# Two linear-attention layers with ReGLU MLPs on one core: another plan of the same work, token tiles of adjacent rows, stores on two queues, a padded weight

## The chip, the cores and the metric

The kernel runs on one core of a Trainium2 chip. The metric is the device time of one execution in microseconds (us); lower is better. The engines are named as in the profile: PE (TensorE's matmuls; PEld is its weight loads), DVE (VectorE), ACT (ScalarE), POOL (GpSimd) and SP (SyncE, which here only issues transfers).

## The reference

The input is a sequence of 2048 tokens of 512 values in bfloat16. Two rounds with the same weights are computed, each an attention block A and an MLP block B with residual additions:

```python
def A(x):                                   # linear attention, H = 32 heads of Dh = 16
    q, k, v = split(x @ wqkv)
    phi = lambda u: concat([softmax(u @ w_phi), softmax(-(u @ w_phi))])   # per head
    kv, z = sum_s phi(k)^T v, sum_s phi(k)
    return (phi(q) @ kv / (phi(q) @ z + 1e-6)) @ wo
def B(x):                                   # MLP, F = 1376
    gate, up = x @ W_gate, x @ W_up
    return (relu(gate) * up) @ W_down
for _ in range(2):
    x = x + A(layernorm(x)); x = x + B(layernorm(x))
```

The sum over all tokens in A means that no query of a round can be finished before all keys of that round are done. Everything else goes token by token.

## The kernel before, in words

**Tiles.** The tokens are cut into 16 tiles of 128 rows (`T`, `P`), which stay in SBUF as X for the whole run. Before the change, four tiles make a group `c`, and partition `p` of the group holds four neighbouring tokens, one in each tile (`xv`, `ov`, lines 285 and 286). A pair of tiles is loaded with one transfer.

**Operations.** Nothing is ordered by loops. The function builds a list of 1855 operations (`op`), numbered by when they are created, each with an engine, what it depends on, and the buffers that it takes and uses. Four tables written out above it hold a plan that was made beforehand: `ORDER` (line 185) is the order in which all of them are emitted, and with it the order in each engine's own queue; `SLOTS` (161) says which buffer of a pool each operation takes; `PLACE` (155) says, for each operation that two engines could do (`alt`), which one does it; `IDLE` (173) puts dummy matmuls ahead of PE operations (the fifth PE operation gets one). `arrange` (76) only replays the plan. An engine works through its queue in order, so an operation that waits holds back all behind it on that engine.

**Stages.** For each tile: load, layer norm statistics (line 500), scaling (522 on POOL, 524 on DVE), transposition (485 by a transfer for a pair of tiles, 490 on PE for a single tile), keys K (581), values V (586), exponentials on ACT (564), their sums on DVE (591), scaling on POOL or DVE (551), and the accumulation over all tokens `kvz` (614). Queries Q (641) go the same way and are transposed by a transfer (666). When all tiles' keys are summed, the state R is built on DVE (626, 631) and the attention of each tile runs: `erq` (677), division (684 to 691), transposition `oT`, output product (700), residual (704). The MLP runs in blocks of 1, 1, 2, 4, 4 and 4 tiles: centring (720), transposition, gate and up products (777; the last 96 of the 1376 columns apart, 753), relu on ACT (781), the product of the two on DVE, either straight from PSUM (794) or after a copy on ACT (796, 785), then the down product (817) and the residual (824). The weights wk and wq are folded with `w_phi` at the start (463, 471).

**The down product.** W_down has 1376 = 10 x 128 + 96 rows, so its 11th slice has 96 rows in `wd`, and the 11th matmul of each tile contracts over 96 partitions (`m`, line 816). The 11th slice of the other operand comes out of a transposition of `hr`, whose last 32 columns are set to zero at the start (`hr0`, line 403).

**Transfers.** All loads, stores and transpositions are issued by SP, but for the load of the first x tile and of w_phi, which ACT issues. They take eight semaphores, the counters, in turn: a transfer can be issued when the one eight places earlier in the list has landed. The first transfers of SP's queue before are: x2, wk (first half), x1, x4-5, wk (second half), x3, wv, wv, x6-7, x8-9, x12-13, wq, wq, then the transposition of tiles 4 and 5, Wq's two, the transposition of tiles 12 and 13, x10-11, x14-15 (xN is the load of tile N). The other weights follow between transpositions. At the end, each tile is stored when its residual is done (890); the last tile in two parts of 384 and 128 columns. The queue of SP ends with a transposition for the last MLP block and then 13 stores.

Of the kernel before, what the change touches and what calls it, by code (L numbers as in the profile page):

```python
# [8 lines left out]
P = 128  # L9
D = 512  # L10
# [135 lines left out]
class K:  # L146
# [9 lines left out]
    "1001001010001001101010000101111000001001111100100001101100111011000011000000100000101111011100010100"  # L156
    "1001101111010010110000010110000011011001111010011101100111110011110011001111111010011101111101011001"
    "1100011011011000110101111111111101111110010101011000010100100001101000100101111100010011011001010100"
    "1010110010011111000100110101101001100101100011101100100"
)  # L160
SLOTS = (
    "0001450332111040002521331020252213134130241204554001324122142118332305232454002133223601357001146113"
    "37331110214c1029215b124e344a030f050d1609305j031g253c321b012i144h204k360a1200050401151502000212011020"
    "2400001150000020350210121400102105010002500401004005212214201851002313115213501425303231310500410142"
    "1024202011521574410443221121100401010352431312302242101240511013402460230322025003051301002510502000"
    "1042222135013132244254224011350135402481030275405k21311041150211321401210232450232222330131532542063"
    "2110112025213310385404e052f313d2459131i320j201b062b154f210c145a3509160h004d212e331g12011301020313001"
    "0124302000035011021540000124501002145001012230210000111041011030210121231001501441322200001041042225"
    "0420351321112001514214224324413412402523105223205102100110050000220551450552131532232412541321040123"
    "1130421000550542551212451342421030015034"  # L170
# [3 lines left out]
    0, 0, 0, 0, 1,  # L174
# [100 lines left out]
)  # L275


@with_exitstack
def kernel(
# [22 lines left out]
    def x_of(t):  # L302
        return X[t // C][:, t % C, :]
# [632 lines left out]
```

## Time and profile before

| what | value |
|---|---|
| time, median of 3 runs | 369.18 us (368.44 to 369.18) |
| profiled execution's own time | 368.89 us |
| its span, first to last instruction | 367.1 us |
| PE busy, matmuls | 360.5 us (98%), 2589 |
| DVE, ACT, POOL busy | 267.8, 188.2, 71.4 us |
| bytes moved by DMA | 31.70 MB |
| granted TensorE clock | 0.999 |

The span is what the trace covers; the time of an execution is a little longer. Busy time is the time in which an engine works on an instruction; waits, and the issuing of transfers, are not in it. A row of a timeline gives the start, the length, the engine with the line, the operation, what it writes and reads, and in brackets the engine's idle time ahead of it with what ended it. A row of groups gives the count, the busy time, the mean of one in ns, and the idle time ahead with what ended it.

### The profile page before, as it was taken

What the parts mean: (1) busy time and instruction counts of PE and PEld (TensorE: products, weight loads), DVE (VectorE), ACT (ScalarE), POOL (GpSimd) and SP (SyncE); (2) the same over time, 40 slices, a digit from 0 to 9 for tenths busy, and PEclk for the clock granted to TensorE, in tenths of its full rate; (3) what the DMA queues carried; (4) which work ended last, traced back from release to release, by engine and by line L of the source; (5) the groups of instructions that cost most, each with busy time, mean ns of one, the idle gap of its engine ahead of it and who ended that gap; (6) DMA issues with size and microseconds to landing.
All of it is one profiled execution on the core that took longest, in us unless ns stands there. A gap on an engine that the chain in (4) does not pass through costs nothing.

```text
span 367.1 us, 6928 instructions
## 1 busy us (share of the span) xinstructions
PE 360.5 (98%) x2589; PEld 199.2 (54%) x2589; DVE 267.8 (73%) x607; ACT 188.2 (51%) x530; POOL 71.4 (19%) x101
## 2 busy tenths in 40 slices
PE   8999999999999999999999999999999999999994
PEld 4445568786545444444544556776755444454442
DVE  6999999998887247958789898899756745251342
ACT  6899998361434633414883375863423441434220
POOL 6579831210010001000208363010300000000000
PEclk9999999999999999999999999999999999999999
DMA  7987776466730600041110206346652210200025
GB/s 246 214 208 203 192 163 130 90 127 134 116 71 18 131 10 3 1 100 30 29 42 3 57 4 145 45 77 147 145 119 57 63 30 0 57 2 14 0 59 173
DMA packets 92994, 31.70 MB, mean 86 GB/s; under 512 B 85184, under 2 KB 91168, under 8 KB 92960
## 3 DMA queue, kind: packets, MB, share of 16 engines
q1 hardware_dynamic: 92288, 31.11, 38.1%
q8 instruction: 20, 0.33, 0.4%
q10 hardware_dynamic: 672, 0.15, 0.2%
q14 instruction: 14, 0.11, 0.1%
HBM read 8.44 MB, written 2.10 MB: 29 GB/s over the span
## 4 chain that ended last, share of the span: by engine, by line
PE 93%; DMA 3%; DVE 2%; issue 0%; ACTq 0%; SPq 0%; ACT 0%
PE b L777 38%; PE b L817 21%; PE b L700 8%; PE b L641 7%; PE b L586 6%; PE b L581 6%; PE b L753 3%; PE q L614 2%; PE q L677 2%; DMA X<-in_A_x_dram 2%; DMA wf<-in_A_w_phi_dram 1%; DVE bstA L500 1%; PE b L490 1%; DVE sk L591 1%; DVE X L824 0%
## 5 line engine op out<-in xcount | busy, mean ns | idle before, releaser
L777 PE MATMUL b<-xnTB,wgu 128*128 128x512 bf16 (+2 forms) x960 | 150.7, 308 | 0.0
L777 PEld LDWEIGHTS <-wgu 128*128 128x128 bf16 x960 | 80.3, 98 | 57.4 <-issue 0.2
L781 ACT ACTIVATE gu<-b 128x512 bf16<-128x512 f32 (+1 forms) x82 | 47.9, 589 | 100.0 <-PE b L777 93.6
L817 PE MATMUL b<-wd,hT 128*128 128x512 bf16 (+3 forms) x363 | 84.1, 372 | 0.0
L564 ACT ACTIVATE ek<-b 128x480 bf16<-128x480 f32 x128 | 68.2, 585 | 11.4 <-PE b L641 7.0
L794 DVE TENSOR_TENSOR hT<-gu,b 128x512 bf16<-128x512 bf16 (+1 forms) x53 | 35.1, 663 | 36.3 <-PE b L777 19.8
L551 POOL TENSOR_TENSOR ek<-ek 128x480 bf16<-128x480 bf16 x40 | 39.2, 1008 | 94.2 <-ACT ek L603 93.9
L817 PEld LDWEIGHTS <-hT 128*128 128x128 bf16 (+1 forms) x363 | 34.5, 98 | 37.4
L591 DVE TENSOR_REDUCE sk<-ek 128x64 f32<-128x960 bf16 x32 | 36.1, 1143 | 1.8 <-ACT ek L564 0.9
L646 DVE TENSOR_REDUCE sq<-ek 128x64 f32<-128x960 bf16 x32 | 36.4, 1144 | 0.0
L662 POOL TENSOR_TENSOR ek<-ek 128x480 bf16<-128x480 bf16 x18 | 18.3, 1020 | 87.2 <-DVE ek L657 56.6
L700 PE MATMUL b<-wo,oT 128*128 128x512 bf16 x128 | 31.4, 379 | 0.0
L586 PE MATMUL b<-wv,xnTA 128*128 128x512 bf16 x128 | 31.4, 379 | 0.0
L824 DVE SCALAR_TENSOR_TENSOR X<-b,rsB,X 128x512 bf16<-128x512 f32 (+2 forms) x33 | 23.8, 727 | 9.0 <-PE b L817 8.6
L581 PE MATMUL b<-Wk,xnTA 128*128 128x480 bf16 x128 | 30.2, 366 | 0.0
L641 PE MATMUL b<-Wq,xnTA 128*128 128x480 bf16 x128 | 30.1, 365 | 0.0
L691 DVE TENSOR_TENSOR o<-q,rd 128x512 bf16<-128x512 f32 x32 | 22.0, 689 | 10.0 <-ACT rd L688 9.7
L785 DVE TENSOR_TENSOR hT<-gu 128x512 bf16<-128x512 bf16 x29 | 12.1, 421 | 21.0 <-ACT gu L796 21.0
L796 ACT CAST gu<-b 128x512 bf16<-128x512 f32 x29 | 17.0, 586 | 16.2 <-PE b L777 15.4
L704 DVE SCALAR_TENSOR_TENSOR X<-b,X 128x512 bf16<-128x512 f32 x32 | 22.0, 686 | 3.5 <-PE b L700 3.3
L500 DVE BATCH_NORM_STATS2 bstA<-X 128x6 f32<-128x512 bf16 x32 | 21.3, 682 | 2.1 <-DMA X<-in_A_x_dram 2.0
L700 PEld LDWEIGHTS <-oT 128*128 128x128 bf16 x128 | 12.2, 98 | 13.2
(77 smaller groups left out, 328.8 us busy)
## 6 DMA issues: line engine op xcount, KB each, us to landing
out_dram<-X SPq DMA_DIRECT2D x15, 128.0 KB, 2.2
X<-in_A_x_dram SPq DMA_DIRECT2D x6, 256.0 KB, 4.7
wgu<-in_B_W_gate_dram SPq DMA_DIRECT2D x4, 344.0 KB, 3.4
wgu<-in_B_W_up_dram SPq DMA_DIRECT2D x4, 344.0 KB, 4.0
wd<-in_B_W_down_dram SPq DMA_DIRECT2D x5, 256.0 KB, 3.9
hT<-in_A_wqkv_dram SPq DMA_DIRECT2D x4, 256.0 KB, 5.3
wv<-in_A_wqkv_dram SPq DMA_DIRECT2D x2, 256.0 KB, 4.5
wo<-in_A_wo_dram SPq DMA_DIRECT2D x4, 128.0 KB, 4.0
```

The source lines that it names most:

```text
L551: e.tensor_tensor(out=v[:, :, 0:DF, :], in0=v[:, :, 0:DF, :], in1=spread(ek, v, n), op=Alu.mult)
L564: nc.scalar.activation(out=pairs(ek, s)[:, :, 0:DF, :], in_=ps.t[:, 0:FW].rearrange("p (b f h) -> p b f h", h=2, f=DF), func=AF.Exp, scale ...
L581: k = op("PE", mm(4, FW), due, lambda: [nc.tensor.matmul(kp.t[:, 0:FW], lhsT=xnTA[c][:, i, b, :], rhs=Wk2[:, b, :], start=(b == 0), stop=( ...
L586: v = op("PE", mm(4, 512), due_v, lambda: [nc.tensor.matmul(vp.t[:], lhsT=xnTA[c][:, i, b, :], rhs=wv[:, b, :], start=(b == 0), stop=(b == ...
L591: a = op("DVE", SUM16, due, lambda: nc.vector.tensor_reduce(out=sk.t[:, row, :].rearrange("p (b h) -> p b h", h=2), in_=summed(pairs(ek)), ...
L641: q = op("PE", mm(4, FW), due, lambda: [nc.tensor.matmul(qp.t[:, 0:FW], lhsT=xnTA[c][:, i, b, :], rhs=Wq2[:, b, :], start=(b == 0), stop=( ...
L646: a = op("DVE", SUM16, due, lambda: nc.vector.tensor_reduce(out=sq.t[:].rearrange("p (b h) -> p b h", h=2), in_=summed(pairs(ek)), axis=AX ...
L700: a = op("PE", mm(4, 512), due + 3, lambda j=j, yp=yp: [nc.tensor.matmul(yp.t[:], lhsT=oT.t[:, j, b, :], rhs=wo[:, b, :], start=(b == 0), ...
L777: nc.tensor.matmul(ps.t[:, q * W:(q + 1) * W].rearrange("p (i t) -> p i t", t=P), lhsT=wgu[:, s, b, g * P:(g + 1) * P], rhs=xT.t[:, 0:n, b ...
L781: nc.scalar.activation(out=gu.t[:, 0, 0:cols], in_=gp.t[:, 0:cols], func=AF.Relu)
L794: nc.vector.tensor_tensor(out=h.t[:, f0 * W:f0 * W + cols], in0=gu.t[:, 0, 0:cols], in1=up.t[:, 0:cols], op=Alu.mult)
L817: nc.tensor.matmul(yp.t[:, 0:c1 - c0], lhsT=h.t[:m, f * W + i * P:f * W + (i + 1) * P], rhs=wd[:m, f, c0:c1], start=(f == 0), stop=(f == N ...
```

## The change

It has four parts.

1. Tile `t` holds the tokens 128 t to 128 t + 127, partition `p` one of them. A pair of tiles is still loaded with one transfer, now of two runs of 1 KB a partition in place of one of 2 KB.
2. The last 32 rows of the 11th slice of `wd` are set to zero by a DVE memset at the start, a new operation (number 25; those behind it move up by one), and all down products contract over 128 partitions and wait for the memset.
3. A store may be issued by ACT or by SP; the choice is in `PLACE`. In the new plan ten of the 17 stores are on ACT and seven on SP. The last eight in emission order are, SP: tile 12, tile 8, tile 14, the last 128 columns of tile 15; ACT: tile 9, tile 13, tile 10, the first 384 columns of tile 15.
4. `ORDER`, `SLOTS`, `PLACE` and `IDLE` are those of another plan, in whose making the eight counters of the transfers were taken into account. The number of matmuls, the dummies among them, is the same.

Read out of the new lists: SP's queue begins x2, x1, wk (first half), x4-5, wk (second half), wv, wv, x3, x12-13, x6-7, x8-9, wq, x10-11, wq, wo (last block), then the transposition of tiles 4 and 5, Wq's first, x14-15, Wq's second. The block weights (`Wblk`, line 419) are built on DVE, not on POOL. The dummy matmul stands ahead of the second PE operation. Behind the folding of wk, PE's first products are V, K of tiles 2, 0 and 1 mixed with V of tile 1, tile 3's turn, V of tile 0, K and V of tile 3, then K of tile 5; before, K of tile 4 came at this place after the same nine products. The first `kvz` stands behind the keys of tiles 12 and 13. In round 2, two query products stand between the last `kvz` and the first `erq` (before: one); in round 1, two query products, a turn and an `erq` stand between the first output product and the first turned MLP tile (before: one query product, a turn and an `erq`).

```diff
-    xv = xf.rearrange("(c p i) d -> c p i d", c=C, i=C)
-    ov = of.rearrange("(c p i) d -> c p i d", c=C, i=C)
+    xv = xf.rearrange("(t p) d -> p t d", p=P)
+    ov = of.rearrange("(t p) d -> p t d", p=P)
...
-        o = load(due, X[t // C][:, t % C:t % C + n, :], xv[t // C][:, t % C:t % C + n, :], n * 131072, eng, follow, t < 1)
+        o = load(due, X[t // C][:, t % C:t % C + n, :], xv[:, t:t + n, :], n * 131072, eng, follow, t < 1)
...
+    wd_zero = op("DVE", dve(D, 4), 9500, lambda: nc.vector.memset(wd[FR:P, NF - 1, :], 0.0), name="wd0", port=True)
...
-                            m = min(P, F - f * P)
-                            nc.tensor.matmul(yp.t[:, 0:c1 - c0], lhsT=h.t[:m, f * W + i * P:f * W + (i + 1) * P],
-                                             rhs=wd[:m, f, c0:c1], start=(f == 0), stop=(f == NF - 1))
+                            nc.tensor.matmul(yp.t[:, 0:c1 - c0], lhsT=h.t[:, f * W + i * P:f * W + (i + 1) * P],
+                                             rhs=wd[:, f, c0:c1], start=(f == 0), stop=(f == NF - 1))
...
-                              [made[f] for f in range(lo, hi)] + l_wd + ([last] if lo else []),
+                              [made[f] for f in range(lo, hi)] + l_wd + [wd_zero] + ([last] if lo else []),
...
-                    op("SP", (460, 1700), e0, lambda t=t, c0=c0, c1=c1: nc.sync.dma_start(
-                        out=ov[t // C][:, t % C, c0:c1], in_=x_of(t)[:, c0:c1]), [a], name="store",
-                       move=256 * (c1 - c0) / RATE)
+                    ways = [(e, (460, 1700), lambda q=q, t=t, c0=c0, c1=c1: q.dma_start(
+                        out=ov[:, t, c0:c1], in_=x_of(t)[:, c0:c1]), False)
+                            for e, q in (("SP", nc.sync), ("ACT", nc.scalar))]
+                    op(*ways[0][:2], e0, ways[0][2], [a], name="store", move=256 * (c1 - c0) / RATE, alt=ways[1])
...
 ORDER = (
-    1, 16, 5, 29, 7, 8, 25, 0, 4, 20, 19, 28, 10, 9, 6, 82, 3, 83, 46, 2, 21, 11, 18, 30, 26, 22, 47, 32, 12, 17, 84,
...
+    1, 16, 5, 30, 7, 4, 20, 22, 25, 18, 21, 19, 0, 26, 8, 10, 9, 3, 83, 2, 47, 6, 84, 65, 48, 31, 27, 14, 66, 28, 33,
...
 IDLE = (
-    0, 0, 0, 0, 1,
+    0, 1,
```

More of the change, by code (lines that the diff above doesn't have):

```diff
@@ L155 @@
 PLACE = (
[L156 to L159, printed above, removed]
+    "1001000111111011000010000100111100001000011010000011101110101011000110000001000000101101011000001100"
@@ L160 @@
+    "0110001001010011111100101011000000111001001000001101100111100001101010011000101100001100000111000001"
+    "1011010110100110100001111011011000111010010010010101010001001100011111110111100000001001111101110110"
+    "001001111010011001101001110101111111111001101010101111010111000011101010"
 )
 SLOTS = (
-    "0001450332111040002521331020252213134130241204554001324122142118332305232454002133223601357001146113"
-    "37331110214c1029215b124e344a030f050d1609305j031g253c321b012i144h204k360a1200050401151502000212011020"
@@ L164 @@
[L164 to L168, printed above, removed]
@@ L169 @@
-    "0420351321112001514214224324413412402523105223205102100110050000220551450552131532232412541321040123"
-    "1130421000550542551212451342421030015034"
+    "0001543042112102002542113023000115435300453012414205023302011148532213102333434443220614217523155121"
+    "08000150024a001c3109124d032b244h052g161k205d020i365a310c235f152e343j10290100020401111302000234011020"
+    "2300001123000020030210120400102131010002200403001004421210201011302514111013311025401624210500320011"
+    "2110325301052112003722221100131221542240331050312501451230550152540280400241122412323032001100114202"
@@ L171 @@
+    "52400250422501351301031110502140205225544012k5334j01121150111321430422342332200212440410251551302045"
+    "0023302141224104580332b320k060h234g104a253c045d115g064b134e323c040h361f212a3339151i00011501020411001"
+    "0120202000001011021040000125301002131001012530210005020000042013150023041111421340201521000142052015"
+    "2520151454210510114112302222413522311200103200421032410210131120411230512210501530250502311235110112"
+    "0031101050542121030250012251221421014230"
 )
```

176 rows, old and new, of the table ORDER are left out of this document.

## The prediction

> **What bounds the kernel now.** I read the page's totals and its 40 slices first, then the chain that ended last, then PE's waits, then the first 20 us and the last 10 us row by row.
>
> ```profile
> span 367.1 us, 6928 instructions
> PE 360.5 (98%) x2589; PEld 199.2 (54%) x2589; DVE 267.8 (73%) x607; ACT 188.2 (51%) x530; POOL 71.4 (19%) x101
> PE   8999999999999999999999999999999999999994
> PE 93%; DMA 3%; DVE 2%; issue 0%; ACTq 0%; SPq 0%; ACT 0%
> ```
>
> TensorE is busy for 360.5 of 367.1 us and makes up 93% of the chain. Only the first and the last slice are not full. The table by stretches says the same more sharply (columns: length, busy PE, PEld, DVE, ACT, POOL, clock, DMA share, GB/s):
>
> ```profile
> 20.00:58.00 38.00, 38.00 (x324) 20.74 (x322) 36.56 (x64) 37.05 (x113) 25.55 (x30) 1.00 0.79 193
> 58.00:220.00 162.00, 162.00 (x1101) 88.74 (x1098) 129.81 (x288) 79.00 (x233) 25.85 (x27) 1.00 0.28 58
> 220.00:234.00 14.00, 13.93 (x161) 8.43 (x159) 11.42 (x25) 9.27 (x25) 3.89 (x4) 1.00 0.52 114
> 234.00:352.00 118.00, 118.00 (x838) 66.97 (x836) 68.40 (x180) 46.55 (x117) 4.36 (x4) 1.00 0.29 60
> ```
>
> From 20 to 352 us PE is idle for 0.07 us by this view, at the granted clock of 1.00 (the ends of matmuls are modelled, so shorter waits show only in the starts, as in part 4). In 20 to 58 us ACT (37.05 of 38.00) and DVE (36.56) are nearly full too, so a late operand there has no spare engine to catch up on. All PE waits that the view of waits lists:
>
> ```profile
> PE q L437 <- PEq L920: 0.8, 1, 0.8
> PE b L490 <- POOL xn L522: 0.5, 1, 0.5
> PE b L471 <- ACT rsA L510: 0.4, 1, 0.4
> PE q L614 <- DVE ek L551: 0.3, 1, 0.3
> ```
>
> So a new order can win only in three places: the start, a few small waits, and the tail after the last matmul. It can lose anywhere. The profiled execution took 368.89 us, 1.79 us more than its span; the three runs have 369.18, 369.18 and 368.44. I sum against 368.89 and carry the 1.79 over; the median is 0.29 us (0.08%) above it.
>
> **Part 1: W_down padded to 128 rows.** These two groups are the last slice of the down products (96 rows) and the others:
>
> ```profile
> L817 PE MATMUL b<-wd,hT 128*128 128x512 bf16 x310 | 77.2, 379 | 0.0
> L817 PE MATMUL b<-wd,hT 96*128 96x512 bf16 x31 | 11.8, 381 | 0.0
> L403 DVE MEMSET hr<- 128x64 uint32 x2 | 0.2, 112 | 0.0
> 354.27 7.65 PE b L817 x38
> ```
>
> Both take the same (379 and 381 ns), and in the chain's last run, 38 down products of which every eleventh has 96 rows take 7.65 us without a break. The columns don't change, so PE gains 0. The added memset writes 512 elements in 32 partitions; by L403's 112 ns for 64 words (256 words here) it is 0.1 to 0.45 us of DVE, before 2 us, where DVE has no tile to work on. The new dependence of every down product on it was met 60 us earlier. Cost 0; without that cover it is the memset's own time.
>
> **Part 2: work moved between engines.** Decoded from the two lists, the copies of V that ACT makes go from 20 to 27 of 32, the copies of Up from 29 to 35 of 82, the query scalings on POOL from 18 to 13.
>
> ```profile
> L443 ACT CAST vext<-b 128x512 bf16<-128x512 f32 x20 | 11.6, 599 | 2.0 <-PE b L586 2.0
> L796 ACT CAST gu<-b 128x512 bf16<-128x512 f32 x29 | 17.0, 586 | 16.2 <-PE b L777 15.4 <-ACT gu L796 0.6
> L662 POOL TENSOR_TENSOR ek<-ek 128x480 bf16<-128x480 bf16 x18 | 18.3, 1020 | 87.2 <-DVE ek L657 56.6 <-issue 25.8 <-ACT gr L758 4.8
> ```
>
> ACT gains about 7 x 0.60 + 6 x 0.59 = 7.7 us and ten stores; POOL loses 5.1. Summing the same way over the first layer's keys and queries alone, ACT, DVE and POOL each change by 1 us or less, so the full stretch (20 to 58 us) is not loaded more. The rest lies where ACT is busy for 79 of 162 us. Cost 0, hidden by that idle ACT; if some of it lay ahead of a product that PE needs next, each copy costs up to 0.6.
>
> **Part 3: the start.** PE's first useful work and the first product that needs a transposed tile from the DMA queue:
>
> ```profile
> 4.64 0.62 PE L463 MATMUL b<-ident,hT 128*128 128x128 bf16 x8
> 9.06 1.03 PE L586 MATMUL b<-wv,xnTA 128*128 128x512 bf16 x4
> 10.02 1.34 SPq L485 DMA_TRANSPOSE xnTA<-xn  x1
> 15.91 0.57 PEld L581 LDWEIGHTS <-xnTA 128*128 128x128 bf16 x4 [0.27 <-DMA xnTA<-xn]
> 15.97 0.97 PE L581 MATMUL b<-Wk,xnTA 128*128 128x480 bf16 x4
> DMA to landing us min/median/max: 2.3/2.7/5.8
> ```
>
> The last row is from the view of the tile xnTA. The first transposition (tiles 4 and 5) is issued at 10.02 and is the one with the longest landing, 5.8 us, so about 15.85; the load of its weights (15.91) names it as the releaser. It lands late because it stands behind loads in SP's queue. In the new list two more loads stand ahead of it: x tiles 10 and 11 (256 KB) and the last block of wo (128 KB). What 384 KB cost is in these stretches:
>
> ```profile
> 6.20:8.70 2.50, 2.13 (x29) 1.63 (x28) 2.50 (x7) 2.49 (x10) 2.30 (x5) 1.00 1.01 338
> 8.70:11.80 3.10, 3.10 (x24) 1.67 (x22) 2.61 (x6) 2.88 (x8) 1.96 (x5) 1.00 1.17 348
> ```
>
> 393 KB at 348 bytes per ns is 1.13 us. The x pairs, 2 KB runs before and 1 KB runs after, add little: the first stretch lands 1 KB runs at 338, the second mostly 2 KB runs at 348, 3% of 0.75 us for each of five pairs, 0.1 us. The transposition then lands near 17.1.
>
> When does PE need it? Both lists have the same nine K and V products and one turned tile between the first V product (9.06) and this point (15.97). Ahead of that, wk's first half is issued one place later and x1 one earlier, DVE builds the block weights instead of POOL, and POOL is freed for the tiles: followed row by row, the first V product comes at 8.9 to 9.0, within -0.2 to +0.5 of before. So PE arrives near 16.0 and **waits 1.1 us**. What goes is the wait of the first kvz, which now stands behind five more products:
>
> ```profile
> 19.45 0.43 PE L614 MATMUL q<-vext,ek 128*128 128x65 bf16 x8 [0.30 <-DVE ek L551]
> ```
>
> The one spare dummy matmul moves from the fifth to the second PE operation, where PE waits for wk in both: 0. The start's net is +1.1 - 0.3 - 0.1 = **+0.7 us**. Bounds: -0.6 (the transposition isn't held up, and the fold is earlier) and +2.6 (it and the next ones each come later, see the rivals). I take the value by the DMA row, since PE runs in order and nothing that it could do meanwhile stands ahead of the waiting product.
>
> **Part 4: two small waits.** Layer 2's first attention product follows the state R, one query product after the last kvz; layer 1's first turned MLP tile follows its centring:
>
> ```profile
> 225.62 0.97 PE L641 MATMUL b<-Wq,xnTA 128*128 128x480 bf16 x4
> 226.67 0.41 PE L677 MATMUL q<-R,fq 128*128 128x68 bf16 x8
> 55.78 0.97 PE L641 MATMUL b<-Wq,xnTA 128*128 128x480 bf16 x4
> 56.72 0.40 PE L490 MATMUL b<-ident,xn 128*128 128x128 bf16 x4
> ```
>
> Four query matmuls occupy 4 x 0.2025 = 0.81 us (480 columns at 2.4 per ns plus 2.5 ns), so PE was late by 226.67 - 226.43 = 0.24 and 56.72 - 56.59 = 0.13. In the new list one more query product stands in the first gap, and one more query in the second. **-0.35 us.** Counting, for each PE operation, the PE work since its last PE ancestor less the durations on the way, the old list has two places with 0.03 us to spare behind the start, the new one has none under 0.3. That speaks against new waits in the middle, but leaves out queueing on ACT and DVE: I hold 0 to +1.5 us for it, and take 0.
>
> **Part 5: the tail.** The last two additions on DVE, and the stores on SP (the second row from the view of line 890, the last one a stretch):
>
> ```profile
> 361.94 0.97 DVE L824 SCALAR_TENSOR_TENSOR X<-b,rsB,X 128x384 bf16<-128x384 f32 x2 [0.39 <-PE b L817]
> L890 SPq DMA_DIRECT2D out_dram<-X x13: 333/420/512, 357.7 to 363.8; - x13
> 357.69 6.47 SPq L890 DMA_DIRECT2D out_dram<-X  x13
> 357.00:366.00 9.00, 5.52 (x36) 2.87 (x34) 3.13 (x5) 0.00 (x0) 0.00 (x0) 1.00 0.54 177
> ```
>
> The last addition ends at 362.91, but the last store is issued at 363.8 (363.75): SP works through 13 stores at 6.47 / 13 = 0.50 us each. After, the last eight stores are split, four on SP and four on ACT. Between the tiles of the last two on SP lie 7 matmuls of 384 and 11 of 128 columns, 1.7 us, so SP is free when the last addition ends and issues within 0.04 us instead of 0.84: **-0.8 us**, bounds -0.5 and -1.1. ACT's four stand behind its last MLP work, with nothing behind them. Its six earlier ones each hold it for about as long as an issue on SP (420 ns); by the list the additions that they wait for come well before, and the transfer eight places earlier, whose counter each of them shares, has landed. ACT is idle enough there (46.55 busy of 118 us).
>
> The Trainium skill speaks against spreading stores: "DMA: Bandwidth & Descriptors", section "Issuing engines are not separate DMA queues", says that issuing from several engines only saves the sequencer's issue time, since all share the same DMA engines. Here the DMA engines are busy for 0.54 of 357 to 366 us, so the trace agrees that the issue is the limit, and by the rule the sum stays at -0.8. If movement were the limit the tail would give 0.
>
> **Sum.** 368.89 + 0.7 - 0.35 - 0.8 = 368.4 us (span 366.65).
>
> **Rivals.**
> - *The transposition is not late* (chance 0.20). The queue's extra loads overlap its wait for its own tile, or land faster. For it: 5.8 us is far over the 2.7 median, so part may be its own. Then the start gives -0.4: 368.89 - 0.4 - 0.35 - 0.8 = 367.3.
> - *The crowded queue costs more than one wait* (0.28), the other side. Behind the first transposition stand Wq's two, with x tiles 14 and 15 (256 KB, 0.75 us) now between them; if the first lands at 19.0 (+3.0) the fold of Wq and the next keys wait too. Start +2.6: 368.89 + 2.6 - 0.35 - 0.8 = 370.3. It decides from a landing of 17.6 on (start +1.15), where the gains are used up. For it: PE has no slack here. Against: 1.13 us by the bandwidth row.
> - *The tail doesn't shorten* (0.12): the stores' movement, not their issue, ends the run. 368.89 + 0.7 - 0.35 = 369.2. Against: 0.54 above.
>
> **How the numbers follow.** Forecast 0.40, rivals 0.20, 0.28, 0.12. About 0.2% (0.74 us) is what a measurement of this kernel tells from no change, so faster means under about 368.4 and slower over 369.9. The forecast lies on that line: half of it counts as faster, half as the same. Faster: 0.20 + 0.20 = 0.40. Same: 0.20 + most of the tail's case, 0.10, less than 0.02 of it slower: 0.29. Slower: 0.28 and the rest, 0.31. Range: the first rival's 367.3 less 0.3 for the tail's bound gives 367.0; the second's 370.3 with a little of the middle's bound gives 370.6. Forecast's own range 367.9 to 369.1.
>
> **What would show it.** The first key product on tiles 4 and 5 waits about 1 us near 16 to 17 for a DMA; the kvz wait is gone; no wait ahead of L677 near 226; the last store is issued within 0.1 us of the last addition and the span ends about 3.4 us after it (now 367.1 - 362.91 = 4.2); PE's busy time stays at 360.5. A PE wait of over 0.3 us anywhere between 20 and 352, or a start over 1.2 us later, proves me wrong.

## The result, and the profile after

The changed kernel takes 367.36 us (median of 13 runs, 366.64 to 368.52), the kernel before 368.83 us beside it (13 runs, 368.28 to 369.18). The ratio is 0.9963, 95% interval 0.9952 to 0.9974: faster by 1.47 us. The profiled execution took 366.92 us. Lines of the changed kernel are one higher than before from L407 to L813.

The totals, PE's slices and the chain of the changed kernel's page:

```profile
span 365.1 us, 6937 instructions
PE 360.0 (99%) x2589; PEld 199.4 (55%) x2589; DVE 266.8 (73%) x613; ACT 190.7 (52%) x540; POOL 62.1 (17%) x93
PE   8999999999999999999999999999999999999996
PE 93%; ACT 2%; DMA 2%; DVE 2%; issue 0%; POOL 0%; POOLq 0%
```

PE still bounds the kernel and its busy time is the same to 0.5 us; the span is 2.0 us shorter. The last slice is fuller (6, was 4). The waits of PE in the changed kernel:

```profile
PE b L582 <- DMA xnTA<-xn: 0.8, 1, 0.8
PE q L438 <- PEq L921: 0.8, 1, 0.8
PE b L464 <- DMA hT<-in_A_wqkv_dram: 0.3, 1, 0.3
PE b L472 <- DVE hT L445: 0.2, 1, 0.2
```

The wait of the first kvz is gone. New are one for a transposed tile and one for W_k's load (hT is the buffer that W_k is loaded into). Where they lie, in PE's rows of the changed kernel:

```profile
5.55 0.62 PE L464 MATMUL b<-ident,hT 128*128 128x128 bf16 x8 [0.35 <-DMA hT<-in_A_wqkv_dram]
8.80 1.03 PE L587 MATMUL b<-wv,xnTA 128*128 128x512 bf16 x4
15.72 0.97 PE L582 MATMUL b<-Wk,xnTA 128*128 128x480 bf16 x4
20.64 1.19 PE L582 MATMUL b<-Wk,xnTA 128*128 128x480 bf16 x5 [0.78 <-DMA xnTA<-xn]
224.73 1.78 PE L642 MATMUL b<-Wq,xnTA 128*128 128x480 bf16 x8
226.35 0.42 PE L678 MATMUL q<-R,fq 128*128 128x68 bf16 x8
```

The key product on tiles 4 and 5 (15.72) does not wait; the one on tiles 12 and 13 (20.64) does. The transposition of tiles 4 and 5 was issued at 10.70 and landed at 14.67. Its view, and that of the load of W_k's first half (issued at 1.66, landed at 5.50):

```profile
L486 SPq DMA_TRANSPOSE xnTA<-xn x1: 1338/1338/1338, 10.7 to 10.7; - x1
DMA to landing us min/median/max: 4.0/4.0/4.0
```

```profile
L351 SPq DMA_DIRECT2D hT<-in_A_wqkv_dram x1: 427/427/427, 1.7 to 1.7; - x1
DMA to landing us min/median/max: 3.8/3.8/3.8
```

Eight query matmuls take 8 x 0.2025 = 1.62 us, so the attention product at 226.35 is on time: the wait of 0.24 is gone. The stretches that answer to those of before:

```profile
20.00:58.00 38.00, 37.36 (x327) 20.75 (x328) 35.99 (x60) 36.53 (x110) 23.90 (x28) 1.00 0.70 177
58.00:220.00 162.00, 162.00 (x1107) 88.87 (x1104) 125.71 (x288) 84.86 (x248) 21.30 (x22) 1.00 0.33 67
220.00:234.00 14.00, 14.00 (x162) 8.59 (x160) 12.65 (x24) 9.92 (x25) 1.93 (x2) 1.00 0.00 1
234.00:352.00 118.00, 118.00 (x832) 66.92 (x830) 70.24 (x189) 42.89 (x113) 1.98 (x2) 1.00 0.35 69
357.00:366.00 9.00, 5.11 (x34) 2.71 (x32) 3.78 (x6) 0.00 (x0) 0.00 (x0) 1.00 0.31 102
```

PE is full from 58 to 352 us, the 0.07 us near 226 included; the DMA's share in the last stretch fell from 0.54 to 0.31, since stores that stood there now go earlier.

The tail of the changed kernel (last additions, the last stores on SP, the last one on ACT; then the view of the very last store):

```profile
361.53 0.96 DVE L824 SCALAR_TENSOR_TENSOR X<-b,rsB,X 128x384 bf16<-128x384 f32 x2 [0.39 <-PE b L817]
358.15 4.71 SPq L890 DMA_DIRECT2D out_dram<-X  x4
362.18 0.34 ACTq L890 DMA_DIRECT2D out_dram<-X  x1
```

```profile
L890 SPq DMA_DIRECT2D out_dram<-X x1: 333/333/333, 362.5 to 362.5; - x1
DMA to landing us min/median/max: 1.5/1.5/1.5
```

The same view of the last store of the kernel before:

```profile
L890 SPq DMA_DIRECT2D out_dram<-X x1: 405/405/405, 363.8 to 363.8; - x1
DMA to landing us min/median/max: 2.3/2.3/2.3
```

The last addition ends at 362.49, the last store is issued at 362.53 and landed at 364.01. Before: 362.91, 363.75, 366.01. From addition to issue 0.84 became 0.04, and from issue to landing 2.26 became 1.48.

**The books of one execution.** PE's lost time is, for each matmul, the distance to the next start less its columns at 2.4 per ns. I sum it over the matmuls that start in the first 40 us ("start") and later ("middle"); "tail" is from the last matmul's start to the end of the span. Before: start 5.09, middle 7.22, tail 4.80. After: 5.21, 6.68, 3.21. So +0.1 - 0.5 - 1.6 = -2.0 us, the difference of the spans. This pair differs by 0.5 us more than the medians (-1.47); why comes out below.

### The profile page after: what moved, and what is told of

Same layout as the page of the kernel before. It is cut to its first block, busy times and chain, and to the rows that moved or that the text cites. A ratio compares the mean times of both kernels' runs of the same rounds, so it can differ in the third digit from the quotient of the medians.

```text
span 365.1 us, 6937 instructions
## 1 busy us (share of the span) xinstructions
PE 360.0 (99%) x2589; PEld 199.4 (55%) x2589; DVE 266.8 (73%) x613; ACT 190.7 (52%) x540; POOL 62.1 (17%) x93
## 4 chain that ended last, share of the span: by engine, by line
PE 93%; ACT 2%; DMA 2%; DVE 2%; issue 0%; POOL 0%; POOLq 0%
PE b L778 38%; PE b L817 21%; PE b L701 8%; PE b L642 7%; PE b L587 6%; PE b L582 6%; PE b L754 3%; PE q L678 2%; PE q L615 2%; DMA xnTA<-xn 1%; DVE bstA L501 1%; DMA X<-in_A_x_dram 1%; ACT ek L565 1%; PE b L491 1%; ACT Wk L444 0%
## 5 line engine op out<-in xcount | busy, mean ns | idle before, releaser
L782 ACT ACTIVATE gu<-b 128x512 bf16<-128x512 f32 x82 | 47.4, 586 | 95.2 <-PE b L778 94.1
L817 PE MATMUL b<-wd,hT 128*128 128x512 bf16 (+2 forms) x363 | 84.1, 372 | 0.0
L552 POOL TENSOR_TENSOR ek<-ek 128x480 bf16<-128x480 bf16 x38 | 36.6, 989 | 129.9 <-DVE ek L552 99.9
L817 PEld LDWEIGHTS <-hT 128*128 128x128 bf16 x363 | 34.4, 98 | 36.7
L795 DVE TENSOR_TENSOR hT<-gu,b 128x512 bf16<-128x512 bf16 (+1 forms) x47 | 31.2, 671 | 31.2 <-PE b L778 22.1
L797 ACT CAST gu<-b 128x512 bf16<-128x512 f32 (+1 forms) x35 | 19.7, 574 | 9.0 <-PE b L778 8.9
L786 DVE TENSOR_TENSOR hT<-gu 128x512 bf16<-128x512 bf16 (+1 forms) x35 | 14.2, 408 | 13.4 <-ACT gu L797 13.4
L663 POOL TENSOR_TENSOR ek<-ek 128x480 bf16<-128x480 bf16 x13 | 12.8, 987 | 40.8 <-DVE ek L658 20.3
```

The costliest lines, as they stand in the source:

```text
L552: e.tensor_tensor(out=v[:, :, 0:DF, :], in0=v[:, :, 0:DF, :], in1=spread(ek, v, n), op=Alu.mult)
L782: nc.scalar.activation(out=gu.t[:, 0, 0:cols], in_=gp.t[:, 0:cols], func=AF.Relu)
L795: nc.vector.tensor_tensor(out=h.t[:, f0 * W:f0 * W + cols], in0=gu.t[:, 0, 0:cols], in1=up.t[:, 0:cols], op=Alu.mult)
L817: nc.tensor.matmul(yp.t[:, 0:c1 - c0], lhsT=h.t[:, f * W + i * P:f * W + (i + 1) * P], rhs=wd[:, f, c0:c1], start=(f == 0), stop=(f == NF ...
```

## The experiments

My first theory: the layout made the landings shorter, so that the first transposition wasn't late (L). Rivals: the second issuing queue shortened the tail's landing too (Q), or the new order did it all (O). Each run's ratio is to the kernel before beside it; an interval behind a ratio is at 95%.

**1. All stores back on SP.**

```diff
-                            for e, q in (("SP", nc.sync), ("ACT", nc.scalar))]
+                            for e, q in (("SP", nc.sync), ("SP", nc.sync))]
```

> The changed kernel with all seventeen stores issued by SyncE, in the changed order; nothing else. Theory Q (the second issuing queue brought the gain of the end: it took the backlog of issues away and shortened the landing of the last store): the eight last stores stand in one queue again, the last store is issued about 0.8 us after the last addition and lands 2.2 us later, so 366.9 + 1.6 = 368.5 us. Theory O (the new order stores earlier tiles sooner, and the layout makes the landing short): the last eight additions end about 0.5 us or more apart, so SyncE at 0.5 us an issue keeps up; last issue at most 0.2 us later than in the changed kernel, 1.5 us to the landing, so 367.0 to 367.2 us.

368.52 us, ratio 0.9973 (0.9959 to 0.9987); profiled 367.96: start 6.14, middle 6.70, tail 3.36. These are its last additions, its stores on SP, and the view of those stores:

```profile
362.48 0.96 DVE L824 SCALAR_TENSOR_TENSOR X<-b,rsB,X 128x384 bf16<-128x384 f32 x2 [0.39 <-PE b L817]
359.10 4.84 SPq L890 DMA_DIRECT2D out_dram<-X  x8
```

```profile
L890 SPq DMA_DIRECT2D out_dram<-X x8: 332/358/445, 359.1 to 363.6; - x8
DMA to landing us min/median/max: 1.5/1.7/1.8
```

SP alone issues eight stores in the time in which it needed to (the last at 363.55, 0.11 us after the addition), and the tail is longer by 0.15 us. In the new order the second queue is worth that much in this profile; O holds for the tail, Q does not. The median is nevertheless the 368.5 that Q forecast and not O's 367.0 to 367.2. The profiled execution, 0.6 us below the median, doesn't have the time in its tail but in its start: with nothing changed there, it is 0.9 us worse than in the first profile of the changed kernel, which neither theory expected. The interval overlaps that of the changed kernel (0.9952 to 0.9974), so the time alone decides nothing.

**2. The old layout in the changed kernel.** `xv`, `ov`, the load and the store are those of before.

> The changed kernel with the tiles' tokens laid out as before (a row of a tile is every fourth token of a block of 512, for loads and stores); order, stores, padding as changed. Theory L (rows of a tile that lie together in memory make the sixteen engines end a transfer together): the loads of two tiles spread from first to last landing by 1.7 us again (1.0 in the changed kernel), the transposition of tiles 4 and 5 lands near 17 instead of 14.7, and the first key product on them waits 1 us or more; the last store lands 2.2 us after its issue begins, not 1.5. Together 367.36 + 0.7 + 1.0, 368.5 to 369.5 us. Rival (the order and the second queue did it, the layout nothing): 367.4 us, transposition at 14.7, last store 1.5 us.

368.37 us, ratio 0.9973 (0.9961 to 0.9985); start 6.56, middle 6.71, tail 3.34. The transposition of tiles 4 and 5 landed at 15.09, 0.88 us after the last load ahead of it (14.21), and PE didn't wait for it. The last store landed 1.65 us after its issue. So in this profile the tail is 0.13 us longer with the old layout, and L falls as the reason why the first transposition is in time. The time decides nothing: the median lies 1.0 us above the rival's 367.4 and just below L's range, and the start of 6.56 is one that the changed kernel itself has (5.21 in its first profile, 6.99 in run 5).

**3. The new layout alone in the kernel before.**

> The kernel before with the layout of adjacent tokens alone, for loads and stores. Theory L: the transposition of tiles 4 and 5 lands 1 us or more earlier than 15.87, the spread of the two-tile loads falls from 1.7 to 1.0 us, the last store lands 1.5 us after its issue begins instead of 2.26; the issue backlog of 0.8 us stays. 368.83 - 0.7 (end) and up to 0.3 less at the start, 367.8 to 368.2 us. Rival (the layout does nothing): 368.8 us, landing of the last store 2.2 us after its issue.

368.68 us, ratio 0.9983 (0.9972 to 0.9995); start 4.62, middle 7.49, tail 4.70. The last store still needs 2.25 us to land, against L. But the transposition of tiles 4 and 5 landed at 13.63 instead of 15.87, as L says. Run 4 shows that this isn't the layout either. Nor does the layout set how far the parts of a load land apart: the sixteen semaphore updates by which the trace tells a landing spread, for pairs of tiles, over 1.0 us here, 1.9 in run 1 with the same layout, and 0.6 in run 4 with the old one. The ratio itself stays below 1, by 0.2 to 1.0 us; what that small gain rests on isn't shown, and on top of the split none is seen (runs 4 and 8 both have 0.9949).

**4. The split of the stores alone, in the kernel before.**

```diff
-                    op("SP", (460, 1700), e0, lambda t=t, c0=c0, c1=c1: nc.sync.dma_start(
+                    by = "ACT" if (t, c0) in ON_ACT else "SP"
+                    q = nc.scalar if by == "ACT" else nc.sync
+                    op(by, (460, 1700), e0, lambda q=q, t=t, c0=c0, c1=c1: q.dma_start(
```

> The kernel before with six of its last thirteen stores (tiles 3, 6, 1, 10, 8 and the first part of 15) issued by ScalarE instead of SyncE; nothing else. The backlog of issues goes under every theory: last issue within 0.1 us of the last addition, -0.8 us. Theory Q adds a shorter landing, 1.5 us instead of 2.26: 368.83 - 1.6 = 367.2 us. Theory L leaves the landing near 2.2 us, since the rows of a tile still lie apart: 368.83 - 0.8 = 368.0 us. A rival of both, that the transfers themselves and not their issue are what is full at the end (the same bytes then land at the same time): 368.8 us.

367.67 us, ratio 0.9949 (0.9930 to 0.9967); start 4.67, middle 7.22, tail 3.42. The issue backlog is gone (last addition 362.49, last issue 362.52) and the landing is 1.65 us, as Q says; the median lies between Q's 367.2 and L's 368.0. With run 1: either cure, the split or the order, takes the tail from 4.8 to about 3.4. And with the old layout and the loads of before, the transposition of tiles 4 and 5 landed at 13.02. In the profile of the kernel before, the same program up to there, it was 15.87. So that 15.87 belonged to one execution. The view of this transposition in run 4:

```profile
L486 SPq DMA_TRANSPOSE xnTA<-xn x1: 1327/1327/1327, 10.2 to 10.2; - x1
DMA to landing us min/median/max: 2.8/2.8/2.8
```

New theory (S): a transposition lands a fixed time after the last load ahead of it, and the profile of before was disturbed there.

**5. The changed kernel again.**

> The changed kernel once more, unaltered, as a second profile of its start and as the measure for the kernels beside it. Theory S (the first transposition lands 0.9 us after the last load that stands ahead of it in SyncE's queue, whatever the execution; the loads themselves land up to 1.2 us apart from one execution to the next): landing of the transposition of tiles 4 and 5 = landing of wo's last block + 0.9 us (14.7 to 15.7), a wait of 0.8 to 1.3 us of the key product on tiles 12 and 13 near 20, ratio 0.995 to 0.998. Rival (the late landing of 15.87 in the kernel before is its own, the changed kernel's start has no such spread): the same rows as in the first profile to 0.1 us.

367.90 us, ratio 0.9969 (0.9959 to 0.9980). The profiled execution took 368.72 us: start 6.99, middle 6.74, tail 3.18. The transposition landed at 15.39, 1.07 us after the last load, as S has it. Less its own start, this execution took 361.73 us and the first one 361.71, so the 1.8 us between these two lie in the start. Its waits of PE, and the row of the second of them:

```profile
PE b L582 <- DMA xnTA<-xn: 1.1, 1, 1.1
PE b L464 <- DMA hT<-in_A_wqkv_dram: 1.0, 1, 1.0
```

```profile
6.20 1.03 PE L464 MATMUL b<-ident,hT 128*128 128x128 bf16 x8 [1.00 <-DMA hT<-in_A_wqkv_dram]
```

W_k's first half landed at 6.15, where it was 5.50 in the first profile and 6.65 in run 1; in every kernel that loads it ahead of tile 1 it landed at 4.33 to 4.59. The first of its sixteen landings came at 4.25 to 4.79 instead of 3.82 to 4.08: on average 0.6 us of the delay are its place, the rest is that the last of the sixteen came 0.65 to 2.1 us behind the first (0.4 to 0.8 with W_k first).

**6. x14-15 behind the transposition of tiles 12 and 13.** In `ORDER`, operation 15 goes behind 259, and 286 and 287 behind 284.

> The changed kernel with the load of x14-15 moved in SyncE's queue from ahead of Wq's second transposition to behind the transposition of tiles 12 and 13, and the statistics of tile 15 moved behind those of tile 14 on VectorE; nothing else. Theory S: the load's 256 KB no longer stand ahead of two transpositions; that of tiles 12 and 13 lands 1 us or more earlier (by 19.5 instead of 20.59), the wait of 0.95 us at 19.64 goes, the whole is 0.6 to 0.9 us shorter than the unaltered kernel beside it. Rival T (transpositions follow one another slowly whatever lies between, or what follows takes the wait over): the wait stays or comes back within 10 us as one for statistics or x14-15, and the time is that of the unaltered kernel to 0.3 us.

367.71 us, ratio 0.9955 (0.9938 to 0.9973); start 6.85, middle 6.71, tail 3.25. Inconclusive as a time. The wait of the key product near 20 went, but one of 1.0 us stood at 25.0, and the view of waits puts it down to the copy of Wq, which is the second half of rival T, that what follows takes the wait over:

```profile
PE b L464 <- DMA hT<-in_A_wqkv_dram: 1.3, 1, 1.3
PE b L582 <- DVE Wq L445: 0.9, 1, 0.9
```

**7. The same, and W_k's first half ahead of tile 1.**

```diff
-    1, 16, 5, 30, 7, 4, 20, 22, 25, 18, 21, 19, 0, 26, 8, 10, 9, 3,
+    1, 16, 5, 30, 7, 20, 22, 25, 18, 21, 19, 0, 26, 8, 4, 10, 9, 3,
```

> As the run with x14-15 later, and the first half of W_k is loaded ahead of tile 1, as in the kernel before. Theory S: W_k's first half lands 0.7 us earlier (4.8 instead of 5.50), the first transposition on TensorE starts 0.5 us earlier or more; if the next wait does not take it over, the whole is 0.3 to 0.6 us shorter than the run beside it. Rival T: the first value product starts at 8.8 us as before, since tile 2's normalisation ends last there, and the time is that of the run beside it to 0.2 us.

366.99 us, ratio 0.9942 (0.9928 to 0.9956), below the changed kernel beside it (0.9969, 0.9959 to 0.9980); start 4.93, middle 6.69, tail 3.19. This is the lowest median of the study; runs 8 and 9 can't be told from it. PE's first product on W_k starts at 4.90 without a wait for its load, and no DMA is among PE's waits:

```profile
4.90 0.61 PE L464 MATMUL b<-ident,hT 128*128 128x128 bf16 x8
6.24 0.40 PE L491 MATMUL b<-ident,xn 128*128 128x128 bf16 x4 [0.73 <-POOL xn L523]
```

**8. The kernel before with the split and the layout, in its own order.** Runs 3 and 4 together.

> The kernel before, in its own order, with two parts of the change: six of the last thirteen stores by ScalarE, and the layout of adjacent tokens. If the order of the work brought only the two small waits (0.4 us) and gave up as much at the start, this kernel is as fast as the changed one: 0.9950 to 0.9965 of the kernel before, a wait of 0.24 near 226 still there, no wait at 20. If the order matters more (rival), it stays 0.5 us or more above the changed kernel.

367.17 us, ratio 0.9949 (0.9937 to 0.9961); start 5.35, middle 7.31, tail 3.25. It has the waits of 0.24 near 226 and 0.13 near 56, one of 0.8 for W_v near 9, and none for a transposition. The median is 0.7 us below the changed kernel beside it (367.90), and the intervals all but part, so it is at least as fast as the whole change. The start is shorter than the 6.99 of run 5 and the middle longer than its 6.74: what the new order gains in the middle it gives back at the start.

**9. W_k's first half ahead of tile 1, alone, in the changed kernel.** The diff of run 7, with 15 left in its place.

> The changed kernel with one load moved: the first half of W_k goes ahead of tile 1's in SyncE's queue, as in the kernel before; x14-15 stays where the change put it. Theory W (the change puts W_k's first half behind tile 1, and there it lands 0.5 to 1.7 us after TensorE is ready): W_k's first half lands by 4.7 us instead of 5.5 to 6.65, the first transposition on TensorE waits less than 0.2 us, and the whole is 0.5 us or more shorter than the changed kernel, ratio 0.9940 to 0.9955; a wait of up to 1 us near 20 stays. Rival X (the place of x14-15 made the gain of the run with both): ratio 0.996 to 0.997.

367.39 us, ratio 0.9946 (0.9932 to 0.9961); start 5.70, middle 6.69, tail 3.21. W_k's first half landed at 4.48:

```profile
L351 SPq DMA_DIRECT2D hT<-in_A_wqkv_dram x1: 418/418/418, 1.2 to 1.2; - x1
DMA to landing us min/median/max: 3.3/3.3/3.3
```

The wait for tiles 12 and 13 is still there (0.91 at 20.18). Landing and median are as W has them. The interval alone still overlaps that of the changed kernel; that of run 7, with the same step in it, doesn't overlap with that of run 5. Against run 7 no difference can be told, so the place of x14-15 stays worth nothing that was measured.

**10. Tile 1 ahead of W_k's first half, in the kernel before.**

```diff
-    1, 16, 5, 29, 7, 8, 25, 0, 4, 20,
+    1, 16, 5, 29, 7, 25, 0, 4, 8, 20,
```

> The kernel before with one load moved: tile 1 goes ahead of the first half of W_k in SyncE's queue, as in the change; nothing else. Theory W: W_k's first half lands at 5.5 to 6.7 us instead of 4.6, TensorE's first transposition waits 0.8 us or more, ratio to the kernel before 1.001 to 1.003. Rival (the wait is only moved: the next step, the normalisation of tile 2, ends as late as before): W_k lands later, and the ratio is 1.000 within 0.001.

370.43 us (368.85 to 371.67), ratio 1.0026 (1.0013 to 1.0040): by the interval this one step costs 0.5 to 1.5 us. Four of the twelve executions had a granted clock of 0.992 to 0.995; the six at 0.999 or more have a median of 369.9, the fourteen such of the kernel before 369.24, so 0.7 us are not the clock's. The profiled execution was the fastest of the twelve and shows the wait for W_k, but its whole start is 5.11, no longer than the 5.09 of the kernel before. The cost is shown by the medians, not by this profile:

```profile
5.71 0.62 PE L463 MATMUL b<-ident,hT 128*128 128x128 bf16 x8 [1.00 <-DMA hT<-in_A_wqkv_dram]
```

**11. x10-11 and W_o's last block ahead of the first transposition, in the kernel before.** The prediction's step by itself: 13 and 304 go behind 323.

> The kernel before with the loads of x10-11 (256 KB) and of the last block of W_o (128 KB) moved in SyncE's queue ahead of the transposition of tiles 4 and 5, nothing else: the step of the prediction on the start by itself. Theory S (a transposition lands about 0.9 us after the last load that stands ahead of it): with 384 KB more at about 350 GB/s its landing comes 1.1 us later than the 13.0 to 14.4 of the same start, at 14.1 to 15.5; TensorE comes for it at about 15.7, so no wait there, ratio 0.9985 to 1.000 (x10-11 is no longer in the way of the second transposition). The prediction's own number (landing at 17.1, a wait of 1.1 us) would give 1.002 to 1.003.

369.10 us, ratio 0.9997 (0.9985 to 1.0008); start 5.73, middle 7.22, tail 4.46. In the profile the transposition landed at 17.08, 2.25 us after the last load (14.83), and the wait that I had predicted is there:

```profile
15.28 1.03 PE L586 MATMUL b<-wv,xnTA 128*128 128x512 bf16 x4
17.13 0.58 PE L581 MATMUL b<-Wk,xnTA 128*128 128x480 bf16 x2 [0.83 <-DMA xnTA<-xn]
```

By the starts it is 0.99 us. Yet the median doesn't move: the ratio is the one that S gave, not the 1.002 to 1.003 of my prediction. But S also gave a landing at 14.1 to 15.5, so by this profile S seems to fail. What the two late landings (15.87 before, 17.08 here) share is in the DMA's queues. Here are the stretches from the last load's landing to the transposition's, first of the kernel before (13.3 to 15.9), then of run 11 (14.9 to 17.1), then of the changed kernel (13.8 to 14.7); the columns are packets, MB and share of 16 engines:

```profile
q1 hardware_dynamic: 980, 0.24, 107.5%
q8 instruction: 1, 0.02, 2.7%
```

```profile
q1 hardware_dynamic: 941, 0.23, 116.0%
q8 instruction: 1, 0.02, 2.9%
```

```profile
q1 hardware_dynamic: 1038, 0.26, 127.8%
```

It is a packet of instructions (program code on its way to an engine), 16 KB, which took 1.11 and 1.01 us (13.80 to 14.91; 15.08 to 16.09). In both, the transposition landed 0.96 and 0.99 us after the packet's end. In these two stretches the data stands nearly still: from 14.6 to 15.6 us in the kernel before and from 15.7 to 16.7 in run 11 the DMA moves 6 GB/s, where the changed kernel moves 286 from 13.8 to 14.7. The other twelve profiles have no such packet there:

| profiles | instruction packet between last load and landing | landing after the last load |
|---|---|---|
| before, run 11 | 1, of 1.0 to 1.1 us | 2.59, 2.25 us |
| the other twelve | none | 0.85 to 1.07 us |

So S holds where no packet of instructions lies between. The twelve have theirs later. In each of the fourteen profiles one packet of 16 KB starts between 13.80 and 17.86 us, and in each, 0 to 1.9 us after that start, data moves at 4 to 16 GB/s for 1.0 to 1.7 us. Run 4 is the kernel before up to here: the packet came at 14.33 to 15.40, when the transposition of tiles 4 and 5 had landed, and the transposition behind it landed at 16.33, 0.93 us after the packet's end and 3.3 us after the one ahead of it (0.96 and 0.88 us in the two profiles of the first row).

**12. Down products over 96 rows again, in the changed kernel.**

```diff
+                            m = min(P, F - f * P)
...
-                            nc.tensor.matmul(yp.t[:, 0:c1 - c0], lhsT=h.t[:, f * W + i * P:f * W + (i + 1) * P],
-                                             rhs=wd[:, f, c0:c1], start=(f == 0), stop=(f == NF - 1))
+                            nc.tensor.matmul(yp.t[:, 0:c1 - c0], lhsT=h.t[:m, f * W + i * P:f * W + (i + 1) * P],
+                                             rhs=wd[:m, f, c0:c1], start=(f == 0), stop=(f == NF - 1))
```

> The changed kernel with the last block of the down projection contracted over its 96 rows again, as in the kernel before (the write of zeros stays); nothing else. If a matmul over 96 rows lasts as long as one over 128, nothing changes: the ratio is that of the changed kernel, 0.9955 to 0.9980, PE's time busy 360.0 us. Rival (the change of the active rows between blocks costs time at each of 33 such matmuls and their neighbours): each such change shows as an excess between matmuls of 10 ns or more, up to 0.6 us in all, and the ratio rises by up to 0.0015.

367.55 us, ratio 0.9956 (0.9941 to 0.9970); start 5.70, middle 6.84, tail 3.26. Its groups of the down products:

```profile
L818 PE MATMUL b<-wd,hT 128*128 128x512 bf16 x310 | 76.4, 379 | 0.0
L818 PE MATMUL b<-wd,hT 96*128 96x512 bf16 x31 | 11.8, 381 | 0.0
```

The middle is 0.15 us longer than in the first profile of the changed kernel; the time is the same. The padding is worth nothing that the time shows.

## Why the prediction was right or wrong

The direction and the range held. The forecast was 1.0 us too high, and 367.36 is below its own range of 367.9 to 369.1. Of that 1.0 us, 0.8 is the tail, whose term was half of what came, and 0.2 the middle. The start came out near its term by luck: it was lost in another place.

- **Parts 1 and 2, cost 0: right.** Run 12 shows it for part 1; for part 2, PE is full from 58 to 352 us with ACT busy for 84.86 of 162 us (79.00 before).
- **Part 3, start +0.7: wrong place, near the right size by luck.** The step that failed is "The transposition then lands near 17.1 ... and waits 1.1 us". It landed at 14.67, PE came for it at 15.72. The base was wrong: I took the 15.87 of one profile as what the queue costs, and about 1.7 us of it (2.59 after the last load instead of 0.9) came with an instruction packet that fell into that transposition. What I took for the price of 384 KB, 1.13 us, is borne out within the scatter: with W_k first, the last load ahead landed at 13.96 and 13.99 with the new loads (runs 7 and 9) and at 12.15 to 13.41, 12.86 on average, with those of before (four executions). The part of it for the layout, 0.1 us for five pairs, was too small: at 0.07 us a pair (last section) it is about 0.35. My step can be seen in run 11, where the packet fell in again: 17.08 and a wait of 0.99.

  What the start really costs is a load that I passed over in half a sentence, W_k's first half "one place later". In the six executions with this order it landed 0.8 to 2.3 us later (5.36 to 6.65 instead of 4.33 to 4.59), and the first V product came at 8.80 to 10.40, in three of the six at 9.9 or later; with W_k first it came at 9.06 to 9.34 where W_v was in time. Runs 7, 9 and 10 show this from both sides. To it comes the wait for tiles 12 and 13 of 0.8 to 1.3 us in all five executions with this order and x14-15 in its place. It is the rival "the crowded queue" in a small form; moving x14-15 out of the way alone brought nothing that was measured. In all five the packet of 16 KB stands ahead of that transposition's landing too, so how much of this wait is the queue's isn't shown. The mean start of those five is 6.12 us (5.21, 6.14, 6.56, 6.99, 5.70), of the four with the order of before 4.93 (5.09, 4.62, 4.67, 5.35): +1.2 us. By the medians it is 0.7 and 1.0: 2.13 us of middle and tail, less the measured gains of 1.47 and 1.11 (369.01 less 367.90 in run 5).
- **Part 4, two waits, -0.35: right.** Both are gone, and the middle is 0.54 us shorter. No new wait of over 0.3 us came after 25 us; the one at 20.64 lies in the stretch in which I had called any such wait proof against me.
- **Part 5, tail -0.8: right mechanism, half the size.** The step that failed is the landing of the last store, which I took to be as long as before. From addition to issue it is 0.84 to 0.04, as forecast. But the span ends 2.6 us after the addition, where I had said 3.4. The other 0.78 us is that landing, 1.48 us instead of 2.26. In the kernel before, an instruction packet fell into it too. These are the stretches from the last store's issue to its landing or a little more, in the kernel before (363.6 to 366.0) and in run 11 (364.3 to 366.2):

```profile
q1 hardware_dynamic: 450, 0.27, 36.7%
q14 instruction: 1, 0.01, 2.4%
```

```profile
q1 hardware_dynamic: 442, 0.27, 45.7%
```

  The packet of the kernel before started 0.43 us after the issue of the last store and took 0.93 us; the store landed 0.90 us after its end. In runs 3 and 10 it started 0.52 us after the issue, and the store took 2.25 and 2.08 us. In run 11 the tail is that of before, on one queue and with the backlog (last issue 0.88 us after the addition), but the packet came only at 367.75, and the store took 1.61 us. In the others no packet came, or it came over 1.1 us after the issue, and the store took 1.48 to 1.65 us. So neither the backlog by itself nor the layout made the landing long, though the layout may have 0.13 us of it (run 2). Nor is it the chance of one execution, as the 15.87 was: with the order of before and one queue, three of four profiles have the packet in the last store. Issued 0.8 us earlier, the last store met a packet only 1.16 and 1.18 us after its issue (runs 4 and 8) or none, and wasn't held up. Also, I gave the split the credit for the 0.8. It would have been enough (run 4), but so is the new order, in which the earlier stores stand earlier (run 1).
- **The rivals.** "The transposition is not late" came true for itself, at 367.3 even near the time, but by a sum with two errors that cancel: its start of -0.4 was not there, and its tail of -0.8 was half of the measured one. "The tail doesn't shorten" is out.

No run moved an instruction packet on purpose. That it delays the transfer in flight is read from fourteen profiles with it in different places. What remains open is why the sixteen landings of W_k's load and of those behind it spread over about 2 us in some executions with this start (runs 1 and 6) and over 0.6 in another (run 12): no packet of 8 or 16 KB of instructions lies in the first 13 us of any profile.

## What to carry to other kernels

Before a landing time goes into a sum, look whether the same program lands it then in a second profile, and whether a packet of instructions lies between: here the 15.87, which one execution had, and the 2.26, which came with such a packet, were each worth 0.7 us or more of the forecast. In SP's queue at the start, put first what PE needs first: one 128 KB load ahead of W_k cost about 1 us (0.5 to 1.5 in run 10), where the new plan gained 0.5 in the middle. And for stores at the end, see that the queue is empty when the last addition ends; an earlier place for the earlier stores does that about as well as a second engine (tails of 3.36 and 3.42 us in runs 1 and 4).

## What the runs showed of the hardware

- Packets of instructions show up among the DMA queues beside those of data: in the changed kernel's page 20 packets with 0.33 MB on q8 and 14 with 0.11 MB on q14. One of 16 KB took 0.9 to 1.7 us in the first 20 us, data moved at 4 to 16 GB/s for 1.0 to 1.7 us during or behind it, and the next transfer to land after its end did so 0.9 to 1.7 us later, in all fourteen profiles. The Trainium skill, "Runtime: NRT & Kernel Launch", section "Instruction fetch mechanics", has the fetch as a DMA of the sequencer's own, in blocks of 16 KiB, with a cost that is mostly hidden. The size agrees for q8 (16 KB a packet), while those of q14 have 8 KB. Whether the cost is hidden for the engine that fetches was not measured here; for a transposition or a last store beside the packet it was not hidden (2.25 and 2.59 us instead of 0.85 to 1.07; 2.08 to 2.26 instead of 1.48 to 1.65).
- Without a packet of instructions between, the first transposition, issued 1.9 us or more before the last load ahead of it landed, came 0.85 to 1.07 us after that load, in twelve executions.
- Two tiles of 256 KB follow one another every 0.75 us in runs of 1 KB (8.92, 9.68, 10.43, 11.19 in the changed kernel) and every 0.68 us in runs of 2 KB (9.66, 10.32, 11.00, 11.70 in run 2), so 0.07 us a pair.
